# Attention, feed-forward and gated MLP on one core: the order planner charges changes of TensorE's tiling where they fall

## The chip, the core and the metric

The kernel runs on one core of one Trainium2 chip. The number that counts is the device time of one execution in microseconds (us); it is taken as the median of several executions. The profile is of one execution, and its times run from the first to the last instruction of the program.

## What is computed

Three blocks in a row, all in 32-bit floating point, for a batch of 4, 12 heads, a sequence of 448, a head dimension of 64 and a model width of 768:

```python
scores = q @ k.T / sqrt(64); scores = cap * tanh(scores / cap)
attn = exp(scores); attn = attn / attn.sum(-1)          # softmax
x = (attn @ v)  # heads side by side: 448 x 768 for each batch element
x = x + relu(layernorm(x) * g @ w_ch1) @ w_ch2           # 768 -> 3072 -> 768
h = relu(x @ w_in); u, v = h[..., :512], h[..., 512:]
out = (u * (w_spatial @ layernorm(v) + b)) @ w_out
```

## The kernel before

**A program that is planned before it is issued.** The kernel does not issue its instructions as it is written. `Recorder.record` notes every operation with a modelled cost in us, and `Program.add` collects them; the products inside one `with prog.group(...)` are one operation that is issued in one piece. `Program.order` gives every operation a due time, and `Program.plan` is a list scheduler: it steps through modelled time, and whenever an engine is free `pick` takes the ready operation with the lowest due time that has room for its buffers (`room`) and is not due more than `AHEAD` = 28 us beyond what TensorE has done so far (`reach`). The list that comes out fixes the order on each engine's queue. Because `record` issues everything from one place, all instructions carry that one line, L538, in the profile; they are told apart by the names of what they write and read.

**Due times.** For TensorE's operations the due time is the sum of the modelled costs of TensorE's operations that stand before it in the order in which the program is written. Other operations are due by who needs them. So the modelled cost of a group shifts the due times of all that comes after it.

**Tilings.** TensorE's array is used whole (128 rows by 128 columns, written 128*128 in the profile) for the big products, and cut into parts for the products of attention, where two or four smaller products run side by side:

- the scores of a pair of heads (`emit_s`): 64*128, into `two` buffers. There are two `two` buffers in the accumulator memory, and each takes one chunk of 128 keys. A pair has three whole chunks: one group takes the first two (called S01 below), one the third (S2).
- the scores of the last 64 keys of two pairs at once (`emit_st`, called st): 64*64.
- the products with the values (`products` in `emit_v`): 128*64. In the first 12 pairs the first two chunks are one group (V01) and the third with the rest another (V23). In the last 12 pairs all chunks are one group, with a 64*64 part (`last_products`) in every second pair.
- the sums over the keys (`ones` in `emit_v`): 128*32 for two pairs at a time, or 128*64 for a pair alone (the last two pairs of batch elements 0 and 1).
- in the spatial product (`sp_units`), six 64*128 products in the middle of a 128*128 group.

Between scores and values ScalarE takes tanh and exp of each chunk (about 1 us each, `es<-two,qsc` and `es<-es,capt` in the profile; for st `hs<-bank,qsc` and `hs<-hs,capt`), and VectorE adds the chunks up for the sums (`es<-es,es` and `es<-es,hs`). A `two` buffer is free again once tanh has read it.

**What is charged for a change of the tiling.** The modelled cost of a product says nothing of tilings. The writer put constants on groups instead, added to the group's cost wherever it comes to stand:

```python
    def group(self, switch=0.0):
        ...
        o[0][0][1] += self.switch
```

S01 and S2 are charged 0.35 us each (later, where the scores are made of split numbers, 0.2, 0.1 and 0.2 for three groups), st 0.1, V01 and V23 0.2 each, the single value group of the later pairs 0.4, a group of the spatial product 0.2; all other groups nothing. The plan itself does not know which tiling TensorE is in.

**The stretches.** From about 4 to 101 us the first 12 head pairs run with hardly anything else for TensorE. From 101 to 375 us the last 12 pairs are interleaved with the first feed-forward product (`h_unit`, 18 whole-array products of 0.2 us in a group). From 375 us on all products are of the whole array, but for the spatial product's two times four groups.

Of the kernel before, what the change touches and what calls it, by code (L numbers as in the profile page):

```python
# [44 lines left out]


AHEAD = 28
SLACK = 0.35
BIAS = 0.1

# [64 lines left out]
class Stage:  # L115


    def __init__(self, prog, tc, name, after=(), side=None):
        self.side = side
        self.tc, self.name, self.after, self.then, self.pools = tc, name, after, [], []  # L120
        self.open = not after
        self.left = 0
        self.pool = None
        for a in after:
            a.then.append(self)
        prog.stages.append(self)

    def begin(self):
        self.pool = self.tc.tile_pool(name=self.name, bufs=1, side=self.side)
        pool = self.pool.__enter__()  # L130
        for p in self.pools:
            for t in p.tiles:
                t.tile = pool.tile(t.shape, t.dt, name=t.name)

    def end(self):
# [10 lines left out]
class Slots:  # L146


    def __init__(self, name, tiles, proto=None, stage=None):
        self.name, self.size = name, len(tiles)  # L150
        self.proto = tiles[0] if proto is None else proto
        self.tiles, self.stage = tiles, stage
        self.bufs = []
        self.changes = 0
# [61 lines left out]
class Program:  # L216
# [6 lines left out]
    def __init__(self, nc):  # L223
        self.ops = []
        self.open = None
        self.soon = set()
        self.at = {}
        self.stages = []
        self.engines = {n: Recorder(self, n, e) for n, e in (
            ("PE", nc.tensor), ("V", nc.vector), ("A", nc.scalar), ("P", nc.gpsimd), ("D", nc.sync))}  # L230
# [11 lines left out]
            return name, 0, 128, c0 // 512 * 512, -(-c1 // 512) * 512  # L242
        return name, p0, p0 + ap.ap[0][1], c0, c1

    def add(self, engine, cost, latency, call, writes, reads):
        o = self.open
        if o is None:
            self.ops.append([[(engine, cost, latency, [call])], writes, reads])
        elif engine == "PE":
            for a in writes + reads:  # L250
                self.at.setdefault((len(self.ops), self.region(a)), o[0][0][1])
            o[0][0][1] += cost
            o[0][0][3].append(call)
            o[1] += writes
            o[2] += reads
        else:
            o[0].append((engine, cost, latency, [call]))
            o[1], o[2] = writes, reads

    @contextmanager  # L260
    def group(self, switch=0.0):


        self.switch = switch
        self.open = [[["PE", 0.0, 0.0, []]], [], []]
        yield
        o, self.open = self.open, None
        o[0][0][1] += self.switch
        self.ops.append(o)

    @contextmanager
# [82 lines left out]
    def plan(self, due):  # L354
# [14 lines left out]
        out = []  # L369
# [21 lines left out]
        def reach():  # L391
            return max(spent + AHEAD, relief)

        def pick(e):


            q = ready[e]
            skipped = []
            found = None
            while q and found is None:  # L400
                d, i, k = heapq.heappop(q)
                if taken[i]:
                    continue
                if d > reach():
                    skipped.append((d, i, k))
                    break
                if k:
                    alt = self.ops[i][0]
                    home = alt[0][0]
                    wait = max(0.0, free[home] - now) if busy[home] else 0.0  # L410
                    for d2, i2, k2 in ready[home]:
                        if not taken[i2] and (d2, i2) <= (d, i) and not k2:
                            wait += self.ops[i2][0][0][1]
                    if alt[k][1] > wait + BIAS:
                        skipped.append((d, i, k))
                        continue
                if not room(i):
                    skipped.append((d, i, k))
                    continue
                found = i, k  # L420
            for x in skipped:
                heapq.heappush(q, x)
            return found
# [5 lines left out]
        while True:  # L429
            for e in ready:  # L430
                if busy[e]:
                    continue
                found = pick(e)
                if found is None:
                    continue
                i, k = found
                taken[i] = True
                out.append((i, k))
                for b in bufs[i]:
                    if b.tile is None:  # L440
                        b.pool.take(b)
                busy[e] = True
                cost, latency = self.ops[i][0][k][1:3]
                if e == "PE":
                    spent += cost
                free[e] = now + cost
                if e == "D":
                    moved = max(moved, now + 1.5) + latency
                    latency = moved + 0.77 - now - cost
                heapq.heappush(events, (now + cost, 0, seq, e))  # L450
                done = now + cost + latency + self.DELAY
                for j, at in succ[i]:
# [18 lines left out]
            else:  # L471
                for b in bufs[x]:
                    b.left -= 1
                    if not b.left:
                        b.pool.give(b)
                        if b.pool.stage is not None and not b.pool.stage.left:
                            for s in b.pool.stage.then:
                                if not s.open and all(not a.left for a in s.after):
                                    s.open = True
                                    out.append((s, None))  # L480
                                    for p in s.pools:
                                        p.changes += 1
        assert sum(k is not None for _, k in out) == n
        return out
# [14 lines left out]
class Recorder:  # L499
# [3 lines left out]
    def __getattr__(self, method):  # L503
# [5 lines left out]
        def record(*args, **kw):  # L509
# [27 lines left out]
            def call():  # L537
                fn(*(put(a) for a in args), **{k: put(a) for k, a in kw.items()})  # L538

            self.program.add(self.name, cost, latency, call, [out], ins)  # L540

        return record

# [2 lines left out]
def attn_ffn_gmlp_kernel(  # L546
# [254 lines left out]
    def emit_s(i, cs):  # L801
# [3 lines left out]
            split_s(i, t, cs)  # L805
            return
        scs = [twos.get()[:, :, 0:S] for _ in cs]
        with prog.group(0.35):
            for c, sc in zip(cs, scs):
                for half in range(2):  # L810
                    r = slice(64 * half, 64 * half + 64)
# [5 lines left out]
    def split_s(i, t, cs):  # L817
# [7 lines left out]
        for c in cs:  # L825
# [6 lines left out]
            with prog.group(0.1 if c == 1 else 0.2):  # L832
# [15 lines left out]
    def emit_st(i):  # L848


        scs = [banks.get()[:, 0:S] for _ in range(2)]
        with prog.group(0.1):
            for j in (i, i + 2):
                t = raws[j]
                for half, sc in enumerate(scs):
# [57 lines left out]
    def emit_v(i, ns=range(4)):  # L913
# [14 lines left out]
            st[i] = s, ps, [[e[:, half] for half in range(2)] for e in E] + [et]  # L928
        s, ps, E = st[i]
        if 3 not in ns:  # L930
            with prog.group(0.2):
                products(i, ps, E, ns)
            return
        x = xts[b][h // 2] if b < 2 else hs.get()
# [4 lines left out]
        with prog.group(0.4 if 0 in ns else 0.2):  # L939
            if i >= 2 * H:  # L940
                products(i, ps, E, range(3))
                if i // 2 % 2 == 0:
# [187 lines left out]
    def sp_units(bs, i, sp, bias):  # L1130
# [6 lines left out]
        with prog.group(0.2):  # L1137
# [673 lines left out]
```

## Time and profile before

| | |
|---|---|
| median of 3 executions | 1019.68 us (1018.27 to 1021.52) |
| span of the profiled execution | 1016.5 us |
| median less span | 3.2 us |
| TensorE busy | 1002.0 us of the span (99%) |
| VectorE, ScalarE busy | 856.2 us, 565.4 us |

Reading it: the span is that of the instructions of one execution; what lies around it in the device time is told only by the difference to the median, 3.2 us, and the forecast is set against the median. TensorE's busy time counts a product until its modelled end, so that products that overlap leave no gap; whether TensorE lost time is seen better from the distance between the starts of its products.

### The profile page before, as it was taken

To read this page: it belongs to the slowest core of one execution; us is meant where nothing else is said; L and a number is where in the kernel's file an instruction comes from. 1 tells how busy PE (TensorE), PEld (TensorE's weight loads), DVE (VectorE), ACT (ScalarE), POOL (GpSimd) and SP (SyncE) were. 2 spreads that over 40 slices of the span, in tenths; PEclk is the share of its full clock that TensorE was granted. 3 is DMA by queue.
4 is the path that set the end of the run, shared out by engine and by line. 5 is a ranking of instruction groups with operands and counts; after the bars stand their busy time and mean duration, and the time that the engine had idled before them with its cause. 6 is when DMAs were issued, how large, how long until landed. Compare 5 with 4: busy or idle time off the path is not lost.

```text
span 1016.5 us, 14927 instructions
## 1 busy us (share of the span) xinstructions
PE 1002.0 (99%) x5056; PEld 825.9 (81%) x5056; DVE 856.2 (84%) x1476; ACT 565.4 (56%) x897; POOL 24.3 (2%) x21
## 2 busy tenths in 40 slices
PE   7999999999999999999999999999999999999998
PEld 2332787787778889999889899999999999998887
DVE  6989998878888779989889989877788777778986
ACT  7999776776667344545566245544465322214553
POOL 0000110000000000000001110000000000000000
PEclk9999999999999999999999999999999999999999
DMA  8454779999999999999684233565799986602402
GB/s 261 154 139 144 256 279 360 359 337 369 338 370 363 358 341 403 409 329 375 244 259 144 50 133 117 165 203 194 236 336 395 337 267 222 192 21 71 132 17 109
DMA packets 132048, 248.71 MB, mean 245 GB/s; under 512 B 21970, under 2 KB 93828, under 8 KB 131972
## 3 DMA queue, kind: packets, MB, share of 16 engines
q1 hardware_dynamic: 131972, 247.76, 70.9%
q8 instruction: 40, 0.66, 0.3%
q14 instruction: 36, 0.29, 0.1%
HBM read 167.70 MB, written 80.01 MB: 244 GB/s over the span
## 4 chain that ended last, share of the span: by engine, by line
PE 75%; DMA 14%; DVE 5%; ACT 4%; issue 1%; SPq 1%; DVEq 0%; ACTq 0%
PE bank L538 50%; PE two L538 25%; DMA w<-in_w_dram 5%; DMA kept_w<-wc 3%; DMA hs<-inv 2%; ACT es L538 2%; DMA qk<-in_qk_dram 1%; DMA h<-hx 1%; ACT hs L538 1%; DVE x L538 1%; DMA inv<-rc 1%; SPq L538 1%; DVE rs L538 1%; DVE wh L538 1%; DVE small L538 1%
## 5 line engine op out<-in xcount | busy, mean ns | idle before, releaser
L538 PE MATMUL bank<-rs,wh 128*128 128x448 f32 x1704 | 357.1, 363 | 2.5 <-ACT hs L538 2.2
L538 PEld LDWEIGHTS bank<-rs,wh 128*128 128x128 f32 x1704 | 318.2, 187 | 29.9 <-ACT hs L538 4.4
L538 DVE TENSOR_TENSOR rs<-hs,rs 128x448 fp32r<-128x448 f32 x159 | 94.8, 619 | 3.7 <-ACT rs L538 3.1
L538 PE MATMUL two<-rs,wh 128*128 128x448 f32 x414 | 92.7, 362 | 0.0
L538 ACT ACTIVATE rs<-hs 128x448 fp32r<-128x448 f32 x118 | 64.5, 569 | 36.8 <-DMA hs<-h 27.6
L538 PEld LDWEIGHTS two<-rs,wh 128*128 128x128 f32 x414 | 77.6, 188 | 5.2
L538 ACT ACTIVATE es<-es,capt 128x896 f32<-128x896 f32 x72 | 73.5, 1062 | 0.0
L538 DVE TENSOR_TENSOR wh<-wr,wh 128x768 fp32r<-128x768 f32 (+2 forms) x72 | 62.0, 863 | 5.3 <-ACT wh L538 5.1
L538 ACT ACTIVATE es<-two,qsc 128x896 f32<-128x896 f32 x62 | 61.1, 1023 | 7.4 <-PE two L538 7.4
L538 PE MATMUL bank<-es,vt 128*64 128x448 f32 x288 | 62.1, 552 | 0.0
L538 ACT ACTIVATE wh<-wr 128x768 fp32r<-128x768 f32 (+2 forms) x57 | 44.1, 773 | 27.0 <-DVE wr L538 12.6
L538 DVE TENSOR_TENSOR es<-es,es 128x896 f32<-128x896 f32 x48 | 51.9, 1082 | 2.3 <-ACT es L538 1.8
L538 ACT ACTIVATE hs<-bank 128x448 f32<-128x448 f32 x60 | 32.3, 540 | 37.8 <-PE bank L538 31.2
L538 PEld LDWEIGHTS bank<-es,vt 128*64 128x64 f32 x288 | 17.4, 136 | 36.6 <-issue 27.1
L538 PE MATMUL two<-qk 64*128 64x448 f32 x168 | 40.7, 591 | 5.7 <-DMA qk<-in_qk_dram 4.2
L538 ACT ACTIVATE wc<-w 128x512 f32<-128x512 f32 x36 | 24.1, 673 | 29.4 <-DMA kept_w<-wc 14.6
L538 ACT ACTIVATE rs<-x 128x448 fp32r<-128x448 f32 x34 | 19.0, 573 | 37.7 <-DVE x L538 36.5
L538 PEld LDWEIGHTS two<-qk 64*128 64x128 f32 x168 | 14.3, 192 | 29.6 <-ACT es L538 15.0
L538 PE MATMUL two<-wh,rs 128*128 128x512 f32 x144 | 35.8, 395 | 0.1
L538 ACT ACTIVATE wh<-wqm 128x768 fp32r<-128x768 f32 x20 | 16.9, 844 | 32.0 <-PE bank L538 20.0
L538 PE MATMUL bank<-rx,whb 128*128 128x448 f32 x144 | 32.7, 362 | 0.0
L538 PE MATMUL two<-rx,whb 128*128 128x448 f32 x144 | 32.7, 362 | 0.0
(232 smaller groups left out, 1873.2 us busy)
## 6 DMA issues: line engine op xcount, KB each, us to landing
hs<-h SPq DMA_DIRECT2D x168, 224.0 KB, 5.8
h<-hx SPq DMA_DIRECT2D x84, 224.0 KB, 4.9
w<-in_w_dram SPq DMA_DIRECT2D x24, 768.0 KB, 6.8
w<-in_w_dram SPq DMA_DIRECT2D x36, 512.0 KB, 6.2
wqm<-kept_w SPq DMA_DIRECT2D x30, 384.0 KB, 6.2
qk<-in_qk_dram SPq DMA_DIRECT2D x24, 448.0 KB, 5.0
h<-hs SPq DMA_DIRECT2D x48, 224.0 KB, 4.0
kept_w<-wr SPq DMA_DIRECT2D x24, 384.0 KB, 7.5
```

Source lines behind the costliest of these rows:

```text
L538: fn(*(put(a) for a in args), **{k: put(a) for k, a in kw.items()})
```

## The change

The constants go. `record` hands `add` the tiling of each product: the rows of its moving operand and the partitions of its output. `add` keeps the list of a group's tilings in `modes` and adds `SWITCH` = 0.17 us to the group's cost for each change inside it. In `plan`, `mode` is the tiling that TensorE's last group ended in; a group that begins in another one occupies TensorE for 0.17 us more of modelled time. And `pick` has a preference on TensorE: the ready group with the lowest due time that has room is noted as `first`, but if it begins in another tiling, the search goes on among groups that are due at most `NEAR` = 3 us after it, and the first of them that is ready, has room and begins in the present tiling is taken in its place. If there is none, `first` is taken. The products, buffers and transfers stay what they are; the other lines of the diff (`space`, `more`, `late`) add options that nothing uses.

```diff
+SWITCH = 0.17
+NEAR = 3.0
...
+    def add(self, engine, cost, latency, call, writes, reads, mode=None):
         o = self.open
+        if mode is not None:
+            seen = self.modes.setdefault(len(self.ops), [])
+            if seen and seen[-1] != mode:
+                o[0][0][1] += SWITCH
+            seen.append(mode)
...
-    def group(self, switch=0.0):
-        self.switch = switch
+    def group(self):
...
-        o[0][0][1] += self.switch
...
+        mode = None
+
         def pick(e):
...
-            found = None
+            found = first = None
             while q and found is None:
                 d, i, k = heapq.heappop(q)
                 if taken[i]:
                     continue
+                if first is not None and d > first[0] + NEAR:
+                    skipped.append((d, i, k))
+                    break
...
+                if e == "PE" and self.modes[i][0] != mode:
+                    first = first or (d, i, k)
+                    skipped.append((d, i, k))
+                    continue
                 found = i, k
+            if found is None and first is not None:
+                found = first[1:]
+                skipped.remove(first)
...
                 if e == "PE":
                     spent += cost
+                    if mode != self.modes[i][0]:
+                        cost += SWITCH
+                    mode = self.modes[i][-1]
...
+            mode = (kw["rhs"].ap[0][1], out.ap[0][1]) if self.name == "PE" else None
+            self.program.add(self.name, cost, latency, call, [out], ins, mode)
...
-        with prog.group(0.35):
+        with prog.group():
```

The last pair of lines is from `emit_s`; `split_s`, `emit_st`, `emit_v` and `sp_units` lose their constants in the same way.

## Rows read from the trace of the kernel before

**Rows 1.** The page, part 1: busy us (share of the span) xinstructions, by engine

```profile
PE 1002.0 (99%) x5056; PEld 825.9 (81%) x5056; DVE 856.2 (84%) x1476; ACT 565.4 (56%) x897; POOL 24.3 (2%) x21
```

**Rows 2.** Busy us (xinstructions) by stretch; then granted clock, DMA share, GB/s

```profile
15.00:101.00 86.00, 84.28 (x418) 26.47 (x419) 78.35 (x127) 84.18 (x110) 0.00 (x0) 1.00 0.54 162
101.00:375.00 274.00, 270.71 (x1469) 214.82 (x1468) 227.95 (x372) 180.05 (x264) 8.93 (x2) 1.00 0.97 338
375.00:1016.50 641.50, 636.73 (x3137) 581.46 (x3135) 543.02 (x967) 292.29 (x514) 14.54 (x10) 1.00 0.63 216
```

**Rows 3.** Timeline of TensorE, first stretch: start us, length us, tiling, xrecords

```profile
25.84 1.77 PE L538 MATMUL two<-qk 64*128 64x448 f32 x8
27.55 1.72 PE L538 MATMUL bank<-es,vt 128*64 128x448 f32 x8
29.20 1.02 PE L538 MATMUL two<-qk 64*128 64x448 f32 x4
30.15 0.97 PE L538 MATMUL bank<-es,vt 128*64 128x448 f32 x4
30.95 0.92 PE L538 MATMUL bank<-hs,vt 128*64 128x448 f32 x4
31.81 1.77 PE L538 MATMUL two<-qk 64*128 64x448 f32 x8
33.51 1.72 PE L538 MATMUL bank<-es,vt 128*64 128x448 f32 x8
35.19 1.02 PE L538 MATMUL two<-qk 64*128 64x448 f32 x4
36.14 0.98 PE L538 MATMUL bank<-qk 64*64 64x448 f32 x8
37.05 0.97 PE L538 MATMUL bank<-es,vt 128*64 128x448 f32 x4
...
38.71 0.96 PE L538 MATMUL bank<-es,ones 128*32 128x448 f32 x8
39.59 1.77 PE L538 MATMUL two<-qk 64*128 64x448 f32 x8
...
42.95 1.02 PE L538 MATMUL two<-qk 64*128 64x448 f32 x4
43.91 0.97 PE L538 MATMUL bank<-es,vt 128*64 128x448 f32 x4
44.71 0.92 PE L538 MATMUL bank<-hs,vt 128*64 128x448 f32 x4
45.46 0.92 PE L538 MATMUL bank<-es,ones 128*64 128x448 f32 x4
...
71.56 0.80 PE L538 MATMUL bank<-wh,onesr 128*128 128x448 f32 x2
```

**Rows 4.** Timeline of TensorE, second stretch, one head pair

```profile
216.26 2.48 PE L538 MATMUL bank<-es,vt 128*64 128x448 f32 x12
...
222.48 14.68 PE L538 MATMUL bank<-rs,wh 128*128 128x448 f32 x72
237.09 2.48 PE L538 MATMUL bank<-es,vt 128*64 128x448 f32 x12
```

**Rows 5.** Waits (us, times, longest): ScalarE from 15 to 101, TensorE after 110

```profile
ACT es L538 <- PE two L538: 1.7, 3, 1.2
PE bank L538 <- ACT hs L538: 2.8, 5, 1.0
```

**Rows 6.** Timelines of ScalarE and VectorE: what the second value products wait for

```profile
28.93 0.72 ACT L538 ACTIVATE hs<-hs,capt 128x448 f32<-128x448 f32 x1
37.37 1.16 DVE L538 TENSOR_TENSOR es<-es,hs 64x448 f32<-64x448 f32 x2
43.10 1.14 DVE L538 TENSOR_TENSOR es<-es,hs 64x448 f32<-64x448 f32 x2
73.36 1.01 ACT L538 ACTIVATE es<-two,qsc 128x896 f32<-128x896 f32 x1 [1.21 <-PE two L538]
```

More of the change, by code (lines that the diff above doesn't have):

```diff
@@ L115, with __init__ @@
 class Stage:
-    def __init__(self, prog, tc, name, after=(), side=None):
-        self.side = side
-        self.tc, self.name, self.after, self.then, self.pools = tc, name, after, [], []
+    def __init__(self, prog, tc, name, after=(), side=None, **space):
+        self.side, self.space = side, space
+        self.tc, self.name, self.after, self.then, self.pools, self.more = tc, name, after, [], [], []
         self.open = not after
@@ L128, in begin @@
     def begin(self):
-        self.pool = self.tc.tile_pool(name=self.name, bufs=1, side=self.side)
+        self.pool = self.tc.tile_pool(name=self.name, bufs=1, side=self.side, **self.space)
         pool = self.pool.__enter__()
-        for p in self.pools:
-            for t in p.tiles:
+        for p in self.pools + self.more:
+            for t in p.late if p in self.more else p.tiles:
                 t.tile = pool.tile(t.shape, t.dt, name=t.name)
@@ L146, with __init__ @@
 class Slots:
-    def __init__(self, name, tiles, proto=None, stage=None):
-        self.name, self.size = name, len(tiles)
+    def __init__(self, name, tiles, proto=None, stage=None, late=()):
+        self.name, self.size, self.late = name, len(tiles) + len(late), list(late)
         self.proto = tiles[0] if proto is None else proto
@@ L227, in __init__ @@
         self.at = {}
+        self.modes = {}
         self.stages = []
@@ L243, in region @@
         return name, p0, p0 + ap.ap[0][1], c0, c1
-    def add(self, engine, cost, latency, call, writes, reads):
+    def add(self, engine, cost, latency, call, writes, reads, mode=None):
         o = self.open
+        if mode is not None:
[3 more added lines that the diff above has]
+            seen.append(mode)
         if o is None:
@@ L481, in plan @@
                                     for p in s.pools:
+                                        p.changes += 1
+                                    for p in s.more:
+                                        p.idle.extend(p.late)
                                         p.changes += 1
@@ L538, in call @@
                 fn(*(put(a) for a in args), **{k: put(a) for k, a in kw.items()})
-            self.program.add(self.name, cost, latency, call, [out], ins)
+            mode = (kw["rhs"].ap[0][1], out.ap[0][1]) if self.name == "PE" else None
+            self.program.add(self.name, cost, latency, call, [out], ins, mode)
         return record
@@ L831, in split_s @@
             k = slice(S + 128 * c, S + 128 * c + 128)
-            with prog.group(0.1 if c == 1 else 0.2):
+            with prog.group():
                 for m, (x, y) in enumerate(((hi, hi), (hi, lo), (lo, hi))):
@@ L851, in emit_st @@
         scs = [banks.get()[:, 0:S] for _ in range(2)]
-        with prog.group(0.1):
+        with prog.group():
             for j in (i, i + 2):
@@ L930, in emit_v @@
         if 3 not in ns:
-            with prog.group(0.2):
+            with prog.group():
                 products(i, ps, E, ns)
@@ L938, in emit_v @@
         width = 64 if len(now) == 1 else 32
-        with prog.group(0.4 if 0 in ns else 0.2):
+        with prog.group():
             if i >= 2 * H:
@@ L1136, in sp_units @@
         pss = [banks.get()[:, 0:S] for _ in bs]
-        with prog.group(0.2):
+        with prog.group():
             for b, ps in zip(bs, pss):
```

## Prediction

> **What bounds the kernel now.** I read the page first: TensorE is busy 99% of the span [rows 1], so the kernel is set by what TensorE does back to back, and an order can only gain where TensorE loses time between products, or where it waits. The windows come next, since the stretches differ. From 15 to 101 us TensorE is busy 84.28 of 86 us and ScalarE 84.18 of 86: two engines are full at once, and VectorE has 78.35. From 101 to 375 us ScalarE has 180.05 of 274 and TensorE 270.71, and from 375 on TensorE 636.73 of 641.5 [rows 2]. So TensorE alone sets the time after 101 us; before, ScalarE stands right behind it. Third I read TensorE's timeline for what a change of the tiling costs, fourth the waits: ScalarE waited for scores 1.7 us in three places between 15 and 101, and of TensorE's waits after 110 us the largest sum is 2.8 us in five places [rows 5].
>
> **What one change of tiling costs.** Two products of half the array start together, so four records are two steps. In the first stretch the clean step is read where one tiling goes on: from 44.71 to 45.46, four records with no change, 0.75 us for two steps, 0.375 a step [rows 3]. The couple of pairs from 25.84 to 39.59 takes 13.75 us. It holds, in steps, S01 4, V01 4, S2 2, V23 4, S01 4, V01 4, S2 2, st 2 (four records start together), V23 4, the 128*32 sums 2 (four at a time): 32 steps, 12.0 us. The 1.75 us left over go with ten changes (each of these ten groups of rows begins one): 0.175 us each [rows 3]. The second stretch gives the same: from one V at 216.26 to the next at 237.09 are 20.83 us [rows 4]. The pair has 6 + 2 + 2 steps of 0.375 (values, sums, st), nine steps of 0.2 (the split scores; 18 products, two at a time) and 72 whole-array products, whose step is 14.4 / 72 = 0.2 us by the row at 222.48 (14.61 us to the next row, less one change): 19.95 us. The rest, 0.88 us, are five changes, 0.176 each.
>
> **How many there are.** Ten a couple in the first stretch make 60 for 12 pairs. In the second stretch a pair with sums has five (value, sums, st, scores, whole array) and the other four (values, their 64*64 part, scores, whole array): 54. The spatial product has two inside each of eight groups: 16. Together 130, times 0.175 is 22.8 us, the most that any order could win back.
>
> **The change part by part.**
>
> *The constants.* Per couple in the first stretch the old ones are 0.35 x 4 + 0.2 x 4 + 0.1 = 2.3 us, where the trace shows 1.75; the new charge is 10 x 0.17 = 1.7. In the second stretch they are 0.5 x 2 + 0.4 x 2 + 0.1 = 1.9 against nine changes, 1.58 measured; now 1.53. The plan's clock for TensorE thus ran ahead of the real one by 0.55 and 0.32 us a couple, over six couples each 3.3 and 1.9 us, and now agrees within 0.05. That costs no time by itself. It moves the moments at which the plan believes a buffer free, and so re-deals close choices (VectorE or ScalarE for a copy, this group or that). What that is worth the trace doesn't show; I bound it by the waits that a re-dealing can dissolve or double, 2.8 us after 110 us [rows 5], so -2.8 to +2.8, and take 0, there being no side that a truer clock must fall on for waits this small.
>
> *Groups that can't move.* The 16 changes of the spatial product, those between values and sums and those into the 64*64 part lie inside a group. Nothing is saved on them. After 375 us every group begins and ends in the whole array, so the preference never speaks.
>
> *The second stretch.* Values, st and scores of a pair are written in one place between two `h_unit` groups and already run as one chain [rows 4]. When a value group is first in line, the next `h_unit` is due later by the whole attention work of the pair: (10 steps of 0.375 and nine of 0.2) 5.55 us, over the 3 us of `NEAR`. So whole-array products aren't taken ahead of it, and after the values no group of their tiling is near. I take 0 here; bound: one change gained or lost a pair, 12 x 0.175 = 2.1 us.
>
> *The first stretch.* Here the preference has something to choose. When V01 ends, S2 of the next pair is first, and V23 of the same pair, of V01's tiling, is due only S2 (and st) later, 0.75 to 1.5 us of steps, inside `NEAR`. It is taken if it is ready. Whether it is, the trace tells pair by pair. For the pair with V01 at 27.55, whose V23 has no sums, the last exp of st ends at 28.93 + 0.72 = 29.65, and the products that read it come 0.8 us into V23 (30.15 to 30.95): V23 could have started at 28.85, before V01 ended at 29.20 [rows 3, 6]. For the pair with V01 at 33.51, which has sums, VectorE's addition ends at 37.37 + 1.16 = 38.53, and the sums come 1.66 us into V23: not before 36.87, long after V01's end at 35.19. For the pair alone, VectorE ends at 43.10 + 1.14 = 44.24; the sums come 1.55 us in: 42.69, just before 42.95 [rows 3, 6]. So it is ready where there are no sums (four pairs of 12, of which I leave out the very first, before which nothing has run ahead) and now and then with a pair alone: I count three and one, four places. In each V01 and V23 run on, and S2 follows. What comes then? S01 of the pair after needs both `two` buffers, and S2 has just filled one that only a tanh of about 1 us frees, so S01 is seldom ready; TensorE takes the next V01. Followed to the same point, S01, V01, S2, V23, S01, V01 has five changes, and S01, V01 and V23, S2, V01, S01 has four. One to two changes saved in each of four places: 0.7 to 1.4 us; I take 1.0.
>
> *Whether it reaches the end.* TensorE's gain there only counts if ScalarE can follow. Its idle time in the stretch is 86 - 84.18 = 1.8 us [rows 2], 1.7 of it waits for scores [rows 5]. A gain of 1.0 fits under it. In exchange S2 starts later, by the steps of V23, 1.5 us. What hides that are the exps of the two chunks before it, about 2 us of ScalarE's work, if the plan places them ahead of the tanh of S2; without that cover ScalarE stands still, and at 73.36 it did: two whole-array products at 71.56 had been placed ahead of an S2, and it sat idle 1.21 us [rows 3, 6]. I take the cover as given, since the plan knows when S2 runs.
>
> The Trainium skill has a rule that speaks against the change: TensorEngine Tiling (Array Packing), section PSUM Bottleneck, says in substance that cutting the array up speeds TensorE but not the emptying of the accumulators, which may become the limit. By that rule nothing saved in the first stretch would arrive, and the sum would be 0 where I take 1.0; the trace has the two engines within 0.1 us of each other there, so it doesn't decide between them.
>
> **The sum.** -1.0 (first stretch) + 0 (second) + 0 (constants) = -1.0 us on the profiled span, 1016.5 to 1015.5; with the 3.2 us between span and median, 1018.7 us. A run of this kernel can't tell less than about 0.3%, 3.1 us, from no change.
>
> **Rivals.**
> - *ScalarE is the limit of the first stretch* (or the order hardly changes, because V23 is seldom ready in the plan's times): 1019.7. For it: 84.18 of 86 us. Against it: 1.8 us idle are left, and some of its copies could go to VectorE.
> - *The preference bites everywhere.* If the truer clock and VectorE have V23 ready at V01's end in every pair, four of ten changes a couple go: 24 x 0.175 = 4.2 us, 1015.5. ScalarE would have to give 4.2 us; it has 1.8, and VectorE could take over about half of its own idle time (86 - 78.35 = 7.65), 3.8, which makes 5.6. Against it: the pair at 33.51 missed by 1.7 us. The same side is reached if the re-dealing dissolves the waits of 2.8 us: 1.0 + 2.8 = 3.8, 1015.9.
> - *Slower: S2 comes too late for ScalarE.* In each of the four places V23 before S2 delays the tanh by up to 1.5 us; if it isn't covered, the row at 73.36 gives the price, 1.2 us. 4 x 1.2 - 0.7 = +4.1: 1023.8. It decides from the point at which S2's delay is longer than the exps that stand before its tanh. For it: ScalarE has no slack to make it up. Against it: the two exps.
>
> **How the numbers follow.** Chances: the forecast 0.40, ScalarE the limit or hardly a change of order 0.12, the preference everywhere or waits dissolved 0.29, ScalarE starved 0.19. The first two lie within 0.3% (1016.6 to 1022.7), so same 0.52, faster 0.29, slower 0.19. The point is that of the likeliest, 1018.7; its own range, with 2.1 and 2.8 us either way rarely both, is 1016 to 1021.5. The range for 8 in 10 leaves out the outer part of either other case, under one in 10 each: 1013.5 to 1024.
>
> **What would show it.** In the timeline from 15 to 101 us some eight-record V01 should be followed by V23 without scores between, in about four pairs, and there should be 4 to 8 changes fewer in that stretch, 54 as before in the next. A change should still cost about 0.175 us. ScalarE's waits for `two` should stay under 1.8 us; if they reach 4 us or more, the starving rival holds. If the second stretch has clearly more or fewer than 54 changes, my reading of the due times is wrong; if the difference lies after 375 us, it is re-dealing and not tilings.

## The result, and the profile after

The kernel became slower: 1028.09 us median of 6 runs (1025.81 to 1030.05) against 1018.97 (1015.48 to 1021.52, 6 runs of before on the same chip), ratio 1.0092, 95% interval 1.0072 to 1.0112. Forecast were 1018.7 us, no change, with a range from 1013.5 to 1024. The profiled execution took 1030.05 us, the longest of the six; its span is 1028.2, 11.7 more than before's, where the medians differ by 9.1.

The page's part 1 of the kernel after, which answers to [rows 1]:

```profile
PE 1009.0 (98%) x5056; PEld 829.1 (81%) x5056; DVE 857.5 (83%) x1482; ACT 562.6 (55%) x890; POOL 19.4 (2%) x22
```

TensorE is busy 7.0 us longer with the same 5056 records, and idle 1028.2 - 1009.0 = 19.2 us instead of 14.5: 4.7 more. Its windows, which answer to [rows 2] (the last one ends with the longer span):

```profile
15.00:101.00 86.00, 82.92 (x402) 25.86 (x402) 76.06 (x120) 82.25 (x108) 0.00 (x0) 0.98 0.51 152
101.00:375.00 274.00, 271.18 (x1461) 212.36 (x1458) 227.63 (x378) 175.96 (x257) 2.65 (x2) 0.99 0.94 330
375.00:1028.00 653.00, 644.80 (x3165) 587.77 (x3163) 547.18 (x974) 296.45 (x518) 15.91 (x11) 1.00 0.63 216
```

Between 15 and 101 us TensorE has 16 records fewer, and the granted clock is under 1.00 in two of the three windows. Where the time went shows best by TensorE's records, numbered from the start; the table gives the start of a record less its start in before, in us (the other kernels are the experiments' below). It is of one execution each: after's is the longest of its six, middle's and late's are 2.8 and 2.5 us under their medians.

| record (us in before) | after | m_before | first | middle | late | undo | neutral |
|---|---|---|---|---|---|---|---|
| 300 (66.8) | 2.44 | 1.32 | 0.94 | 0.66 | 0.76 | 1.64 | 0.87 |
| 393 (84.8) | 2.98 | 1.95 | 1.13 | 0.99 | 0.90 | 2.16 | 0.57 |
| 500 (110.4) | 4.10 | 9.51 | 1.28 | 0.87 | 0.94 | 2.20 | 0.58 |
| 561 (122.4) | 3.97 | 9.17 | 0.97 | 1.36 | 1.33 | 2.43 | 0.24 |
| 600 (130.7) | 8.25 | 9.17 | 0.97 | 5.36 | 1.33 | 2.43 | 0.24 |
| 1750 (338.9) | 7.71 | 10.49 | 1.98 | 3.86 | 1.60 | 2.58 | 0.60 |
| 2000 (390.9) | 10.05 | 8.44 | 1.12 | 2.73 | 4.14 | 5.72 | 4.42 |
| 3000 (596.1) | 11.40 | 8.48 | 1.93 | 3.86 | 4.90 | 6.50 | 9.09 |
| last (1012.6) | 11.68 | 8.88 | 2.42 | 3.95 | 5.71 | 6.84 | 9.50 |

After is 3.0 us late at 85 us, loses 1.1 more by 110, 4.3 between 122 and 131, 2.3 between 339 and 391, and 1.4 by 596. Differences of 1 to 2 us in this table can be the execution's own: first, which has after's order up to some 80 us, is 1.13 late at 85 us where after is 2.98, and late, which has before's order until 270 us, is 1.60 late at 339. Of TensorE's 661 groups only 57 stand at another place in after's order, but VectorE, ScalarE and SyncE were dealt anew almost everywhere. Three places follow.

**First: V23 of pair 10 behind st(24).** TensorE's timeline of before, rows that stand in no group ahead of the prediction:

```profile
86.97 0.97 PE L538 MATMUL bank<-es,vt 128*64 128x448 f32 x4
...
90.13 2.00 PE L538 MATMUL bank<-qk 64*64 64x448 f32 x4
92.48 0.97 PE L538 MATMUL bank<-qk 64*64 64x448 f32 x4 [0.35 <-DMA qk<-in_qk_dram]
```

and of after:

```profile
87.34 1.72 PE L559 MATMUL bank<-es,vt 128*64 128x448 f32 x8
89.00 1.02 PE L559 MATMUL two<-qk 64*128 64x448 f32 x4
...
91.52 0.96 PE L559 MATMUL bank<-qk 64*64 64x448 f32 x2 [0.58 <-ACT hs L559]
93.41 0.97 PE L559 MATMUL bank<-qk 64*64 64x448 f32 x4 [0.93 <-DMA qk<-in_qk_dram]
94.31 1.76 PE L559 MATMUL bank<-es,vt 128*64 128x448 f32 x4
```

In before V23 of pair 10 (86.97) comes ahead of the 64*64 products st(24), in after behind them (94.31), and they wait for buffers and a load. The values of pair 10 stand at the head of a chain: sums, their reciprocals by way of transfers to DRAM and back, the scaling, the accumulation, the mean of batch element 1 and its layer norm, of which six rows on VectorE are read by the first `h_unit` of batch element 1. The last of these rows in after, and the last two in before:

```profile
130.44 0.68 DVE L559 SCALAR_TENSOR_TENSOR rs<-hs,g_t,rs 128x448 fp32r<-128x448 f32 x1
```

```profile
123.12 1.26 DVE L538 SCALAR_TENSOR_TENSOR rs<-hs,g_t,rs 128x448 fp32r<-128x448 f32 x2
```

In before the `h_unit` runs while its last two rows are still being made; TensorE's timeline:

```profile
122.82 3.98 PE L538 MATMUL bank<-rs,rs 128*128 128x448 f32 x18
```

In after it starts at 131.18, right behind st(28) and without a wait of its own (next rows). So what the move of V23 costs in after is read from the table, 1.1 us between 85 and 110 us; in middle, which has the same move, it is nothing (0.99 and 0.87). The chain is late as well, but no row shows that TensorE waits for it.

**Second: st(28) right behind S2.** TensorE's timeline of after:

```profile
130.28 0.97 PE L559 MATMUL bank<-qk 64*64 64x448 f32 x4 [2.51 <-DMA qk<-in_qk_dram]
131.18 5.49 PE L559 MATMUL bank<-rs,rs 128*128 128x448 f32 x18
```

In before st(28) comes 18 us after S2 and waits for nothing. In after it stands directly behind it, and the load for its second pair goes into the buffer that S2 has just read, so it could only be issued at 126.91. And the `h_unit` takes 5.49 us where the same one takes 3.98 in before: the granted clock is down. The wait and the clock are the 4.3 us that after loses between 122 and 131 us; middle loses 4.0 there. The clock was down three times (windows of after; columns as in [rows 2], the granted clock is the third number from the end):

```profile
94.40:97.40 3.00, 3.00 (x10) 0.95 (x12) 3.00 (x6) 3.00 (x6) 0.00 (x0) 0.50 0.03 2
131.90:135.20 3.30, 3.30 (x10) 2.98 (x9) 2.43 (x4) 3.30 (x6) 0.10 (x1) 0.50 0.50 149
381.10:384.40 3.30, 3.30 (x11) 2.94 (x10) 2.20 (x3) 1.42 (x2) 0.00 (x0) 0.50 1.05 274
```

0.50 is 1.2 instead of 2.4 GHz. What such a stretch costs the rows tell: 1.5 us on the `h_unit` (5.49 for 3.98), 1.6 on the rows near 381 below (3.62 and 1.65 where before has 2.27 and 1.36). At that price three of them are an estimated 4.7 of the 7.0 us that TensorE is busy longer. Before has none until its last half us.

**Third: the start of the products after attention**, whose weight tiles are `whm`, made from the load `wqm`. After's timeline, then before's:

```profile
379.47 0.67 PE L559 MATMUL two<-rs,whm 128*128 128x448 f32 x2 [1.93 <-ACT whm L559]
380.46 3.62 PE L559 MATMUL two<-rs,whm 128*128 128x448 f32 x10 [0.32 <-DVE whm L559]
383.88 1.65 PE L559 MATMUL bank<-rs,whm 128*128 128x448 f32 x6
```

```profile
371.01 0.67 PE L538 MATMUL two<-rs,whm 128*128 128x448 f32 x2 [0.70 <-ACT whm L538]
372.00 2.27 PE L538 MATMUL two<-rs,whm 128*128 128x448 f32 x10 [0.32 <-DVE whm L538]
374.12 1.36 PE L538 MATMUL bank<-rs,whm 128*128 128x448 f32 x6
```

TensorE's waits after 110 us, which answer to the second row of [rows 5], and ScalarE's from 15 to 101, to the first:

```profile
PE bank L559 <- DMA qk<-in_qk_dram: 2.5, 1, 2.5
PE two L559 <- ACT whm L559: 1.9, 1, 1.9
PE bank L559 <- DVE qkg L559: 1.5, 1, 1.5
PE bank L559 <- ACT hs L559: 0.6, 1, 0.6
```

```profile
ACT es L559 <- PE two L559: 3.0, 4, 1.6
```

The waits that I had named as what a re-dealing can dissolve fell from 2.8 to 0.6 us. Two others came that before doesn't have there, for the load of qk and for `qkg`, and the one for `whm` grew from 0.7.

### The profile page after: what moved, and what is told of

Its sections match the earlier page's. It is cut to its first block, busy times and chain, and to the rows that moved or that the text cites. A ratio compares the mean times of both kernels' runs of the same rounds, so it can differ in the third digit from the quotient of the medians.

```text
span 1028.2 us, 14918 instructions
## 1 busy us (share of the span) xinstructions
PE 1009.0 (98%) x5056; PEld 829.1 (81%) x5056; DVE 857.5 (83%) x1482; ACT 562.6 (55%) x890; POOL 19.4 (2%) x22
## 4 chain that ended last, share of the span: by engine, by line
PE 80%; DMA 10%; DVE 6%; ACT 1%; SPq 1%; issue 1%; POOL 1%; ACTq 0%; DVEq 0%; POOLq 0%
PE bank L559 55%; PE two L559 25%; DMA w<-in_w_dram 3%; DMA qk<-in_qk_dram 1%; DVE x L559 1%; DMA hs<-inv 1%; DVE wh L559 1%; DVE small L559 1%; SPq L559 1%; DVE rs L559 1%; POOL qkg L559 1%; DMA h<-hx 1%; DMA x<-x 1%; DMA inv<-rc 0%; DMA hs<-h 0%
## 5 line engine op out<-in xcount | busy, mean ns | idle before, releaser
L559 ACT ACTIVATE wh<-wr 128x768 fp32r<-128x768 f32 (+2 forms) x52 | 39.9, 767 | 28.4 <-PE bank L559 10.5
L559 ACT ACTIVATE hx<-bank 128x448 f32<-128x448 f32 x34 | 18.5, 544 | 40.2 <-PE bank L559 38.8
```

## The experiments

Times are medians; the ratio, with its 95% interval, is to before, run on the same chip in the same batch, and is not exactly the quotient of the medians. The medians of before were 1018.95 us for the parts, 1017.75 for the rules and numbers, 1019.18 for the moves, 1019.64 for the splices and 1018.65 for the transfers. Where an expectation speaks of theory C, it is this: before's order is one of many, good by having been chosen, and any other deal of the same work costs. Theory D is the chain behind V23 of pair 10.

**The parts of the change, each alone.** The kernel is after's, with the old constants put back in `group`. Two switches choose, for the plan's clock and for the due times, between the new charges (`True`) and the constants (`False`), and `NEAR` = -1.0 turns the preference off. The lines of the first kernel; the others set these three values otherwise:

```diff
-NEAR = 3.0
+NEAR = -1.0
+CLOCK_NEW = True
+DUE_NEW = True
...
+        self.clock[len(self.ops)] = g[1] + (inner if CLOCK_NEW else switch)
+        g[1] += inner if DUE_NEW else switch
...
-                    if mode != self.modes[i][0]:
+                    cost = self.clock[i]
+                    if CLOCK_NEW and mode != self.modes[i][0]:
                         cost += SWITCH
```

New charges in due times and clock, no preference: 

> The new charges alone: constants gone, 0.17 us for each change of tiling in the plan, no preference for the present tiling. Theory A (the re-dealing by the new charges carries the loss): +7 to +11 us against the kernel before. Theory B (the preference carries it, by delaying what ScalarE and the layer norm wait for): -2 to +2 us. Theory C (rugged: any other order lands anywhere, and parts don't add): some other value, such as +4.

The preference alone, with the old constants: 

> The preference alone: the old constants stay in due times and in the plan's clock, no charge for changes of tiling, TensorE takes groups of its present tiling that are due within 3 us. Theory A: -2 to +2 us. Theory B: +7 to +11 us. Theory C: some other value, and the sum with the charges alone is not that of the whole change (+9.1).

The plan's clock alone: 

> Half of the charges: the plan's clock for TensorE takes 0.17 us a change in place of the constants, due times keep the constants, no preference. If theory A holds by the plan believing TensorE earlier than it did (0.55 us a couple of pairs): +5 to +11 us. If it holds by due times: -2 to +2 us.

The due times alone: 

> The other half of the charges: due times without the constants (0.17 us for a change inside a group), the plan's clock as before, no preference. If theory A holds by due times: +5 to +11 us. If by the clock: -2 to +2 us. Theory C: both halves lose or gain something and don't add to the charges alone.

| kernel | us | ratio |
|---|---|---|
| charges (both, no preference) | 1033.21 | 1.0143 [1.0113, 1.0173] |
| preference alone | 1028.26 | 1.0093 [1.0065, 1.0121] |
| clock alone | 1031.37 | 1.0112 [1.0073, 1.0152] |
| due times alone | 1029.92 | 1.0102 [1.0062, 1.0142] |

Any part costs what the whole costs, or more, and they don't add: 14 for the charges and 9 for the preference make 9 together. Charges and clock alone lie above the bands that theory A gave them. So no one part is at fault; what they have in common is that the plan comes out otherwise.

**Rules and numbers in the plan.** Two rules hold a group back until another is taken, and the work is planned again; two more change one number.

```diff
+            if i in held and not taken[held[i]]:
+                return False
```

After, st(24) not ahead of V23 of pair 10: 

> The changed kernel with one rule more: the st group of the 13th couple's place (pairs 12 and 13) may not go before V23 of pair 10, as it does not in the kernel before; all that follows is re-planned. Theory D (V23 of pair 10 starts the longest chain of the stretch: its sums, three transfers, the layer norm of the second batch element, the first h_unit of it; a late V23 delays all): 4 to 8 us of the 9.1 come back, +1 to +5 against the kernel before. Theory C (rugged, any other order costs this much): +6 to +12.

Before, V23 of pair 10 not ahead of st(24): 

> The kernel before with the one rule turned round: V23 of pair 10 may not go before that st group, as in the changed kernel; constants as before, no preference, the rest re-planned. Theory D: +5 to +9 us, and in the trace the first h_unit of the second batch element some 6 to 8 us later. Theory C: anything from 0 to +12 without that place in the trace.

Before with `AHEAD` 27.9 instead of 28: 

> The kernel before with a touch that has nothing to do with tilings: AHEAD 27.9 in place of 28. TensorE's sequence stays the same, VectorE's, ScalarE's and SyncE's change in places, buffers are dealt differently. Theory D (TensorE's order around V23 of pair 10 decides): -2 to +2 us. Theory C: +5 to +12 us, as with every other touch so far.

After with `SWITCH` 0.25: 

> The changed kernel with SWITCH at 0.25 us in place of 0.17. In its order V23 of pair 10 goes ahead of that st group. Theory D: 0 to +4 us against the kernel before. Theory C: +6 to +12. If the preference and the charges are worth anything by themselves once V23 is early, it is below 0.

| kernel | us | ratio |
|---|---|---|
| after, held | 1027.92 | 1.0092 [1.0059, 1.0125] |
| before, held | 1032.86 | 1.0143 [1.0115, 1.0171] |
| before, `AHEAD` 27.9 (neutral) | 1027.97 | 1.0093 [1.0062, 1.0123] |
| after, `SWITCH` 0.25 | 1033.24 | 1.0150 [1.0120, 1.0181] |

The neutral one is the plainest. TensorE's order is the same, operation by operation; only VectorE, ScalarE and SyncE are dealt otherwise in places. Until 339 us it runs with before (0.60 late in the table). Then its longest wait from 300 to 500 us:

```profile
PE two L570 <- ACT whm L570: 3.6, 1, 3.6
```

and the clock falls (its window 374.60 to 377.90):

```profile
374.60:377.90 3.30, 3.05 (x9) 2.52 (x9) 1.76 (x3) 1.18 (x2) 0.00 (x0) 0.50 1.04 277
```

A change of 0.1 in a number that has nothing to do with tilings costs the 9 us of the change. Holding V23 by rule in before and `SWITCH` 0.25 cost 15 us, more than either theory allowed. Holding st(24) in after wins nothing, and theory D missed: V23 ran early, TensorE was 0.3 us ahead of before at record 561, and then st(28) waited 2.8 us for its load all the same; the `h_unit` started at 128.16.

**One move in a finished order.** Nothing is planned again; a group and what hangs on it are moved on TensorE's queue alone.

```diff
+MOVE = ('v', 20), ('st', 24)
...
-        for i, k in self.order():
+        for i, k in self.moved(self.order()):
```

In before, V23 of pair 10 behind st(24): 

> One local move in the finished order of before, nothing planned again: V23 of pair 10 stands behind the products st(24) on TensorE's queue; the orders of VectorE, ScalarE, GpSimd and SyncE are those of before. Theory D (what follows V23 of pair 10, down to the layer norm of batch element 1 and its first h_unit, sets the time between 90 and 135 us): st(24) waits as in the kernel after and ends about 94; V23 of pair 10 runs some 6 us later than in before; the first h_unit of batch element 1 some 5 to 7 us later; the time is 4 to 8 us over before's, 1023 to 1026. Rival C (there is slack of 6 us behind V23 of pair 10; what costs is the re-dealing as a whole): 0 to +2 us, 1019 to 1021.

In after, st(24) behind V23 of pair 10: 

> The same move the other way in the finished order of after: st(24) alone is moved right behind V23 of pair 10; every other engine's order is after's. Theory D: V23 of pair 10 runs near 88 us, no stretch at granted clock 0.5 near 94, and the time is 3 to 5 us under after's, 1022 to 1025; what is left over before is the wait of st(28) and of the start of y_seven. Rival C: as after, 1027 to 1029.

The first gave 1026.69 us against 1019.18, 1.0078 [1.0059, 1.0098]: one move, 7.5 us, inside what theory D said and far from the rival's 0 to 2. Its timeline of TensorE:

```profile
90.86 0.96 PE L590 MATMUL bank<-qk 64*64 64x448 f32 x2 [1.87 <-ACT hs L590]
93.11 2.75 PE L590 MATMUL bank<-qk 64*64 64x448 f32 x6 [1.29 <-ACT x L590]
95.80 1.45 PE L590 MATMUL bank<-es,vt 128*64 128x448 f32 x4
...
105.46 1.02 PE L590 MATMUL two<-qk 64*128 64x448 f32 x4 [2.26 <-ACT es L590]
...
132.00 3.98 PE L590 MATMUL bank<-rs,rs 128*128 128x448 f32 x18
```

V23 runs 8.8 us later (95.80 for 86.97), the `h_unit` 9.2 (132.00 for 122.82). But that is not the chain at work: by the table TensorE is 9.5 us late at 110 us, before the chain reaches the `h_unit`, and loses nothing more after it. The time is lost around the move. ScalarE, whose queue was dealt for an early V23, stood still for the copy of its sums, with the exps of later pairs behind it:

```profile
98.83 0.54 ACT L590 ACTIVATE hs<-bank 128x448 f32<-128x448 f32 x1 [5.77 <-PE bank L590]
```

TensorE waits 6.1 us between 88 and 106 us (1.87, 1.29, 0.67 and 2.26) where before waits 1.2, and its clock fell twice:

```profile
93.50:96.70 3.20, 3.20 (x10) 0.68 (x10) 1.05 (x2) 0.00 (x0) 0.00 (x0) 0.50 0.01 4
107.20:110.40 3.20, 3.20 (x10) 0.73 (x6) 1.59 (x3) 3.20 (x6) 0.00 (x0) 0.50 0.62 191
```

4.9 us of waits and two stretches at 1.6 us are 8.1, against the 7.6 by which the lateness grows from 85 to 110 us. So D's number came true by another mechanism than D's. The second move gave 1027.68, 1.0088 [1.0071, 1.0106], 8.5 over before: the rival's band, and hardly anything came back, against D's 3 to 5 us. V23 ran at 88.08, but its sums then stood still 3.4 us, st(28) waited for its load as in after, and the `h_unit` began at 131.70, again right behind it. The waits of this kernel:

```profile
PE bank L590 <- DVE x L590: 3.4, 1, 3.4
PE bank L590 <- DMA qk<-in_qk_dram: 3.3, 2, 2.4
```

VectorE's queue had been dealt for a late V23: its copy `x<-bank`, which frees the sums' buffer, stands at 92.88. An order that suits one engine's plan is laid down on all.

**TensorE kept at work.**

```diff
+                    for half, sc in [*enumerate(scs)] * FILL.get(i, 0):
+                        r = slice(64 * half, 64 * half + 64)
+                        T.matmul(out=sc[place(j)], lhsT=t[r, S + TAIL:2 * S], rhs=t[r, 0:S], start=True, stop=True)
```

> After's order, with six more products of the tiling 64*64 in st(28), before those of its second pair, written to a place that the pair's own products overwrite: TensorE works while it waits for that pair's load. If the granted clock falls because TensorE stood idle for those 2.5 us: the clock is 1.00 from 131 to 135 and the time is about 1.5 us under after's, 1026 to 1027. Rival: the clock falls there all the same, 1028.

1026.09 us, 1.0076 [1.0055, 1.0098]. The windows of it:

```profile
126.80:130.30 3.50, 2.64 (x14) 1.35 (x11) 3.50 (x8) 3.50 (x6) 1.30 (x1) 1.00 0.22 77
131.00:135.00 4.00, 4.00 (x21) 3.74 (x20) 3.73 (x6) 4.00 (x7) 0.00 (x0) 1.00 0.76 239
```

The clock stays at 1.00 where it fell in after. It is 6.9 us over before where after is 9.1 over; that fits the expected 1.5, but the intervals overlap, so the clock is shown and the saving only fits. **Other numbers for the whole change:** 

> The whole change with other numbers: SWITCH 0.172, NEAR 1.0, AHEAD 32, SLACK 0.302. Theory C (any other order of this planner is a new draw, before's is one that had been found good): anywhere from before's time to 14 us over it, 1018 to 1033. Rival (the change itself costs what it was measured at): about +9 us, 1027 to 1029.

1030.29, 1.0118 [1.0098, 1.0138]: inside C's wide band, above the rival's. It doesn't wait for `whm`; it waits 2.3 us for the load of qk behind S2, as eight of the nine new plans do (all but the neutral one).

**Splices of the two finished orders.** After these twelve runs it was open which stretch of the order costs the time. Each kernel issues one fixed list on all engines. The cuts are where TensorE has issued the same groups in both orders.

```diff
+        for e, x, k in ORDER:
+            if e != "G":
+                assert room(x)
+                out.append((x, k))
```

> Before's finished order on every engine, except that the first 46 of TensorE's 661 groups (up to some 80 us), and what the other engines were given by then, stand in after's order. If the stretch around pair 10 sets the loss: 0 to +2.5 us (after's records ran 2.4 us late at 67 us, half of that may be given back), 1019 to 1021.5. Rival, any mixture of orders costs what a re-dealing costs: +7 us or more, 1026.

> Before's finished order, with groups 47 to 74 (some 80 to 147 us: V23 of pair 10 behind st(24), st(28) right behind S2) in after's order on every engine. If the stretch around pair 10 is the cause: +5 to +8 us, 1024 to 1027. Rival, the loss is spread over the whole order or lies after 270 us: 0 to +3, 1019 to 1022.

> Before's finished order for the first 128 groups (some 270 us), after's for the rest (start of y_seven with the load of wqm behind the kept_w stores, the wait for qkg near 597 us). If the middle stretch is the cause: +1 to +4 us, 1020 to 1023 (after's own records lost 2.3 us at 371 to 384 and 1.4 at 597). Rival, the start of y_seven is the cause: +6 or more, 1025, as in the neutral re-dealing, which lost 7.6 us there with TensorE's order kept.

> After's finished order, with groups 47 to 74 in before's order on every engine. If the stretch around pair 10 is needed for the loss: 5 to 8 us of the 9 come back, 1020 to 1023. Rival, other stretches cost as much once it is mended (st(28)'s load, the start of y_seven): 1025 to 1028.

| after's order in | us | ratio |
|---|---|---|
| groups 1 to 46 (first) | 1019.62 | 0.9999 [0.9986, 1.0012] |
| 47 to 74 (middle) | 1025.23 | 1.0053 [1.0035, 1.0072] |
| 129 to 661 (late) | 1026.50 | 1.0072 [1.0047, 1.0097] |
| all but 47 to 74 (undo) | 1025.13 | 1.0047 [1.0028, 1.0066] |

The first part, which holds most of the stretch that the preference was to serve, costs nothing and gives nothing. The middle alone costs 5.6 us, inside the expected band, and its longest wait after 110 us names the load behind S2. No kernel was run with st(28) alone moved, so that its place is the whole of the middle's cost is read from rows and table, not shown by a run:

```profile
PE bank L559 <- DMA qk<-in_qk_dram: 2.3, 1, 2.3
```

The late part alone costs 6.9, the rival's band and not that of the stretch around pair 10, with this wait:

```profile
PE two L559 <- ACT whm L559: 2.7, 1, 2.7
```

TensorE's order in late differs from before's only between 566 and 593 us. So the loss of 2.5 us between 339 and 391 us that the table gives for it comes with TensorE's order as in before, from how the other engines were dealt. Middle and late don't add: 5.6 + 6.9 = 12.5, and the whole costs 9.1. Groups 75 to 128 of after's order stand in none of the three; undo, which has them, is no slower than late. Taking the middle out of after (undo, 5.5 over before) gives back 3.6 of the 9.1, less than the 5 to 8 of the theory, and leaves about the rival's time. The table by records suggests how they overlap. TensorE comes to the products after attention when its own work is done, and they start when `whm` is there; the later of the two counts. In middle TensorE is 3.9 us late at 339 us and waits 0.3 us there; in late it is 1.6 late and waits 2.7; in after it is 7.7 late and still waits 1.9. Lateness from the middle would then hide a part of the lateness of `whm`.

**What holds `whm` up.** From 150 to 430 us the 16 DMA engines have a busy share of 0.91 to 1.05 in all these kernels, in windows of 25 to 60 us. That they set the arrival of `wqm` was the last theory. Two copies from DRAM to DRAM in before, and two loads left out of late:

```diff
+COPIES = 1102, 1177
...
+            if i in COPIES:
+                self.copy(COPIES.index(i))
```

```diff
+LEFT_OUT = 1102, 1177
...
-            for call in self.ops[i][0][k][3]:
+            for call in self.ops[i][0][k][3] if i not in LEFT_OUT else []:
```

> Before, with two copies of 0.79 MB each from one place in DRAM to another behind two loads of w near 240 and 260 us; nobody waits for them and all else is as before. At the 360 GB/s of that stretch they are 4.4 us of the DMA engines. If the DMA engines set the arrival of wqm: its first load is issued 3 to 5 us later than in before, TensorE waits 3 to 5 us for whm near 371 and its clock falls there, and the time is 4 to 7 us over before's, 1023.5 to 1026.5. Rival, the DMA engines have slack: 0 to +1, with no wait for whm over 1 us.

> The late splice, with two loads of w (0.79 MB each, near 240 and 260 us) left out; what reads them finds older data in the tile, so the numbers of the output change and the work of the other engines doesn't. If the DMA engines set the arrival of wqm: it comes 3 to 4 us sooner, the wait for whm falls from 2.7 us to under 0.7 and no half clock follows: 3 to 5 us under the late splice, 1021.5 to 1023.5. Rival, the order of the instructions around the start of y_seven costs by itself: as the late splice, 1025 to 1027.5.

More transfers: 1022.59, 1.0037 [1.0020, 1.0053], 3.9 us for 4.4 us of DMA work, a little under the band. But not by the wait that was expected: there is none for `whm`. The second copy was issued at 264.86; TensorE waited near 286 us, and the clock fell there (timeline, then window):

```profile
285.67 0.47 PE L541 MATMUL bank<-rs 64*128 64x448 f32 x1 [1.56 <-ACT hx L541]
...
288.29 12.02 PE L541 MATMUL bank<-rs,wh 128*128 128x448 f32 x46 [1.75 <-ACT hs L541]
```

```profile
287.00:293.80 6.80, 5.51 (x15) 4.90 (x16) 5.11 (x9) 5.81 (x8) 0.00 (x0) 0.50 1.03 400
```

This execution is the longest of the ten, and it was 3.8 us late at 131 us already, long before the copies, with a stretch at granted clock 0.50 near 11 us; from there it lost 5.0 by 339 us and gave 2.2 back by the end. So what more transfers cost is shown by the medians: nearly as much as the DMA engines need for them, and the rival, slack in the DMA engines, is out. Whether it is the 16 engines that have none, or SyncE's queue, on which the copies stand as well, isn't told apart. Fewer transfers: 1023.92, 1.0037 [1.0019, 1.0056], 5.3 over before where late is 6.9 over, with intervals that overlap, and above the expected band. And the mechanism failed: `whm` was waited for 3.7 us, and SyncE issued the load of `wqm` at the same time. SyncE's timeline of late:

```profile
352.00 0.53 SPq L559 DMA_DIRECT2D sum<-hs  x1
...
361.02 0.84 SPq L559 DMA_DIRECT2D rc<-sum  x1
...
368.22 1.74 SPq L559 DMA_DIRECT2D wqm<-kept_w  x4
```

of late with the loads left out:

```profile
368.15 1.75 SPq L560 DMA_DIRECT2D wqm<-kept_w  x4
```

and of before:

```profile
350.02 0.54 SPq L538 DMA_DIRECT2D sum<-hs  x1
...
355.98 0.59 SPq L538 DMA_DIRECT2D rc<-sum  x1
...
363.92 1.32 SPq L538 DMA_DIRECT2D wqm<-kept_w  x3
```

Between `sum<-hs` and `rc<-sum` lie 6.0 us on SyncE's queue in before, with nine other transfers, and 9.0 in late, with fourteen; `wqm` follows 7.9 and 7.2 us after `rc<-sum`. That the order of this queue sets the late part is what the rows suggest; no kernel was run with SyncE's order alone changed, so it stays open.

## Why the prediction was wrong

**The step that failed** is the one on the constants: "I bound it by the waits that a re-dealing can dissolve or double, 2.8 us after 110 us [rows 5], so -2.8 to +2.8, and take 0, there being no side that a truer clock must fall on". A new deal is not bounded by the waits that the old one has. It can make new ones where the old had none: measured +9 to +15 us in each of nine plans that were made anew (four parts, two rules, two with another number in after, one with another number in before), none at or under before. The terms for the preference failed in the same way: they were sized by changes of tiling alone (-1.0, bound 2.1), and the preference alone cost 9.3. There was a side to fall on: each order that was tried is worse than the one that was there. Why that one is so good, by a choice among many or by luck, the runs don't show. Of the chances, the 0.19 for slower went to a starved ScalarE, none of it to a worse deal.

**What made it dear** is "So TensorE alone sets the time after 101 us". Being busy 270.71 of 274 us TensorE stands at the end of the paths, but three others had no slack to speak of: the queues of ScalarE and VectorE, dealt to fit TensorE's order (one group moved on TensorE's queue alone, ScalarE stood still 5.8 us, and it cost 7.5), the loads that SyncE issues just ahead of their readers (2.5 us for st(28), and the half clock behind it), and the transfers, whose share of 0.97 stood in the same row of [rows 2] and was not read (4.4 us of them more cost 3.9).

**Point by point.** What one change of tiling costs held: the rows of S2 and V01 in after have the lengths of [rows 3], 1.02 and 1.72 us. Their number, forecast as 130 and 4 to 8 fewer, is 131 in before and 132 in after; up to 110 us 60 and 59. The preference hardly speaks: one run of 20 records of 128*64 at 52.3 us, where four places were forecast. The splice first has two changes fewer in its stretch, by 0.175 each 0.35 us, and takes before's time: the term of -1.0 was too large, and what is left of it can't be measured, nor told from nothing, as the rival that ScalarE is the limit there had it. The second stretch, taken as 0, is where most of the loss is, though not by tilings (57 changes for 55 from 110 us on). ScalarE's waits for `two` rose from 1.7 to 3.0 us, under the 4 at which the starving rival was to hold; its 1023.8 had the right sign by another mechanism. My last sign, a difference after 375 us, was set too late: by 339 us 7.7 of the 11.7 us were lost, by re-dealing.

**Sizes.** Middle 5.6, late 6.9, overlap 3.4, first 0: that is how the 9.1 us are made up, with an uncertainty of some 2 us on each; the overlap is what is left over, and no run measures it. The half clock is in it, not beside it. That a new deal costs is shown; what makes the late part dear stays open.

## What to carry to other kernels

A planner's cost that is made truer is not a small edit: before pricing it, ask what the present order is worth against other orders of the same planner, and try one neutral touch of a number. When one engine is full, look for loads that land just ahead of their readers, and for queues (SyncE, the DMA engines) that are as full as it is: a group that is moved for the sake of 0.175 us can hold up the queues that were dealt to fit it, here by 7.5 us. If the order is good, move single groups in the finished list; a move on one queue alone, though, doesn't undo a plan, since the others are dealt to fit it.

## What the runs showed of the hardware

A wait can cost TensorE more than itself. In after the granted clock was 0.50 for a while right behind waits of 0.6 and 0.9 us in a row, of 2.5 and of 1.9 us, and it cost 1.5 and 1.6 us in the two places where rows can be compared. Where products filled most of the wait of 2.5 us it stayed at 1.00. Not every wait is followed by it. The preference alone waited 3.0 us for qk, and the `h_unit` behind it ran at full speed:

```profile
129.71 0.97 PE L570 MATMUL bank<-qk 64*64 64x448 f32 x4 [3.04 <-DMA qk<-in_qk_dram]
130.61 3.91 PE L570 MATMUL bank<-rs,rs 128*128 128x448 f32 x18
```

The splice first waited 2.1 us near 245 us, and its clock stayed at 1.00 as well. So the length of a single wait doesn't tell. The Trainium skill, TensorE: Matmul & The Clock Gate, section HAM oscillation — how this bites in real kernels, tells of a kernel that waits for transfers and finds the array at the lower clock each time it goes on. The windows agree on the lower level, 0.50, but not on each time.

The clock goes with a part of the spread of runs. Of the late splice's ten runs the quickest, 1020.62 us, had a mean granted clock of 1.000, and the longest, 1032.86, one of 0.995; the first splice, with 0.999 to 1.000 in all ten, ran from 1017.06 to 1020.78. But a mean of 0.995 is an estimated 5 us of lost clock (0.005 of the run), not the 12 between these two, and the neutral kernel's six runs, all at 0.997 or 0.998, lie between 1022.16 and 1031.80.
